# A sparse-attention and gated-feed-forward kernel on one core: conversions issued behind two copies, and the upper weight half taken first

## Chip, core and metric

The kernel runs on one core of one Trainium2 chip. The metric is device time in microseconds (us) of that core, as a median of runs; lower is better.

## What is computed

The reference is an attention with a local window and a few global keys, and a feed-forward layer with a sigmoid gate behind it. Cut to what matters:

```python
# q, k, v: (4, 8, 768, 64) fp32; n_global = 8, n_local = 96
scores = q @ k.T / sqrt(64) - slope[h] * dist      # dist by position
scores = where(is_global | is_local, scores, -1e9)
a = softmax(scores)                                # with + 1e-9 in the denominator
x = (a @ v) laid out as 3072 tokens x 512
gate = 1 / (1 + exp(-(x @ w_gate)))                # 512 x 1536
val = x @ w_val                                    # 512 x 1536
out = (gate * val) @ w_out                         # 1536 x 512
```

## The kernel before

The 3072 tokens are cut into 8 blocks of 384 (`bi` 0 to 7, three 128-token tiles `t` each), the 8 heads into 4 pairs (`s` 0 to 3), the 1536 inner columns into 12 groups of 128 (`f` 0 to 11).

**Attention of a block**, for each pair `s` and tile `t`: `scores` puts two matmuls into two PSUM banks (L373 in blocks 0 and 1), VectorE adds the distance table and takes the row's bound (L406, result in a tile `work`), ScalarE takes the exponential (L419). `transposes` turns the 128x128 probability pieces on TensorE into a bank (L452: `ps_t` and `ps_o0` in turn), and copies the bank to a tile `pT` in SBUF: in block 0 on ScalarE for t = 0 (L457), on VectorE for t = 1 and 2 (L455). `values` multiplies the three `pT` of a pair with v (L502), going through t in the order 2, 1, 0. Tiles `pT` come from a ring of three (`PTB = 3`). In block 0, `pair_out` then normalises into `hh` (L538) and splits it into a rounded `xh` and a rest `xl`; for the last pair ScalarE writes `xh` (L544) and VectorE `xl` (L545).

**Feed-forward**, `ff_in`: a group `f` has a gate half and a value half, in banks `ps_g` and `ps_u`. Each adds 12 matmuls (L564): for 4 chunks `c` of the 512 inputs the three products `w1l*xh`, `w1h*xl`, `w1h*xh`. `w1h` is the rounded upper half of the weight, `w1l` the rest. The gate half is read by ScalarE (L572, tanh), which frees `ps_g` for the next group; the value half by VectorE (L578 or L581). `ff_out` multiplies with the output weight (L604) into three banks `ps_o`.

**Weights** come as 64-bit numbers and are turned to fp32 by integer arithmetic while block 0 runs. `conv_a` issues, on ScalarE, the low bits (L192: `bits`, or `w2f` for the output weight) and two clipped parts of the high word (L199: `neg`, `top`), or for the output weight the latter on VectorE (L203, L206). `conv_b` joins them on VectorE (L180 `top`, then L212 `bits`, or L214). `conv_c` rounds the upper half on ScalarE (L235 `w1h`), and GpSimd takes the rest (L180 `w1l`). Each group f of block 0 needs its `w1h` and `w1l`.

**Order.** A program-level scheduler places instructions by its own estimate of times. `issue_after(later, earlier)` adds an order between two instructions of one engine without a wait. In `conv_a` the first instruction on ScalarE already stands behind the last exponential issued, the first on VectorE behind the last L406. All that the change touches lies in the first fifth of the run: attention of block 0 ends at about 36 us, and block 0's feed-forward, with block 1's attention between its groups, at about 135 us.

Of the kernel before, what the change touches and what calls it, by code (L numbers as in the profile page):

```python
# [28 lines left out]
def attn_moe_kernel(ctx, tc, qT, kT, v, n_global, n_local, wg, wv, wo, out, B, H, S, D):  # L29
    nc = tc.nc  # L30
    DM = H * D
    NC = DM // P
    NF = wo.shape[0] // P
    NPAIR = H // 2
    NTB = S // P
    TB = 3
# [25 lines left out]
    def issue_after(later, earlier):  # L62
        tc.add_manual_dep(
            later.ins,
            earlier.ins.name,
            mybir.DependencyInfo(mybir.DependencyClass.NoSync, mybir.DependencyReason.DATA),
            reason="issue order",
        )
# [91 lines left out]
    w1h = [wpool.tile([P, 2, NC, P], F32R, name=f"w1h{f}") for f in range(NF)]  # L160
    w1l = [wpool.tile([P, 2, NC, P], F32R, name=f"w1l{f}") for f in range(NF)]
# [17 lines left out]
    def sub(eng, out, a, b):  # L179
        eng.tensor_tensor(out, a, b, op=ALU.subtract)  # L180

    def conv_a(j):

        c = conv[j]
        raw, n = c.pop("raw"), c["n"]
        m32 = raw.bitcast(U32).rearrange("p (n t) -> p n t", t=2)[:, 0:n, 1]
        w3 = raw.rearrange("p (n f) -> p n f", f=4)[:, 1:n + 1, 0]  # L190
        c["bits"] = w2f[c["f"]] if c["i"] == 1 else wraw.tile([P, n], I32, name="bits", bufs=2)
        first = nc.scalar.activation(c["bits"], m32, AF.Copy, scale=2.0 ** -13)  # L192
        if last_exp:
            issue_after(first, last_exp[-1])
        c["top"] = top = wraw.tile([P, 2 * CW], I16, name="top", bufs=TOPB)[:, 0:n]
        neg = wraw.tile([P, 2 * CW], I16, name="neg")[:, 0:n]
        if KINDS[c["f"]][c["i"]] == "B":
            for dst, sign in ((top, 1.0), (neg, -1.0)):
                ins = nc.scalar.activation(dst, w3, AF.Relu, scale=8.0 * sign, bias=-8.0 * 14336.0)  # L199
                issue_after(ins, first)  # L200
            sub(nc.vector, top, top, neg)
        else:
            first = nc.vector.tensor_scalar(neg, w3, -18432.0, -14336.0, op0=ALU.max, op1=ALU.min)  # L203
            if last_min:
                issue_after(first, last_min[-1])
            nc.vector.scalar_tensor_tensor(top, w3, 14336.0, neg, op0=ALU.max, op1=ALU.add)  # L206

    def conv_b(j):
# [59 lines left out]
    PAIR = 1  # L268
# [11 lines left out]
    def x_of(bi):  # L280
        o, size = xslot[bi]
        return [x[:, o:o + size].rearrange("p (c n) -> p c n", c=NC) for x in xall]

    steps = {}

    KINDS = ["RR"] + ["BR"] * 11
    TOPB = 1
# [63 lines left out]
    def bank(*names):  # L351

        i = turns.get(names, 0)
        turns[names] = i + 1
        name = names[i % len(names)]
        pool = {"ps_s": ps_a, "ps_t": ps_a, "ps_v": ps_a, "ps_g": ps_gv, "ps_u": ps_gv}.get(name, ps_o)
        return pool.tile([P, 4 * P], F32, name=name)
# [82 lines left out]
    def transposes(bi, s, t):  # L440
        st = steps[bi, s]
        b, t0, nt = blocks[bi]
        n = 1 if t0 + t == 0 else 2
        sb, _ = st.pop(("s", t))
        if bi > PAIR:
            st["pT"][t] = transposes_by_dma(s, n, sb)
            return
        pt = bank("ps_t", "ps_o0") if bi < PAIR else bank("ps_t")
        pt = pt.rearrange("p (c x) -> p c x", c=4)
        for j in range(2):  # L450
            for c in range(n):
                nc.tensor.transpose(pt[:, n * j + c], sb[:, j, c * P:(c + 1) * P], ident)  # L452
        pT = spool.tile([P, 4, P], F32, name="pT", tag="pT", bufs=PTB)
        if bi < PAIR and t > 0:
            nc.vector.tensor_copy(pT[:, 0:2 * n], pt[:, 0:2 * n])  # L455
        else:
            nc.scalar.copy(pT[:, 0:2 * n], pt[:, 0:2 * n])  # L457
        st["pT"][t] = pT

    def transposes_by_dma(s, n, sb):  # L460

        m = 2 * n
        halves = late["pool"].tile([P, 2 * 4 * P], I16, name="halves")[:, 0:2 * m * P]
        words = sb[:, :, 0:n * P].bitcast(I16).rearrange("p j (x h) -> p j x h", h=2)
        for h in range(2):
            dst = halves[:, h * m * P:(h + 1) * m * P].rearrange("p (j x) -> p j x", j=2)
            nc.vector.tensor_copy(dst, words[:, :, :, h])
        turned = late["pool"].tile([P, 2 * 4, P], I16, name="turned", bufs=2)[:, 0:2 * m]
        nc.sync.dma_start_transpose(turned, halves)
        return turned  # L470
# [83 lines left out]
    def ff_in(bi, f, mid=None):  # L554
        b, t0, nt = blocks[bi]
        n = nt * P
        xh, xl = x_of(bi)
        pss = []
        for i in range(2):
            ps = ps_gv.tile([P, NB], F32, name=("ps_g", "ps_u")[i])  # L560
            k = 0
            for c in range(NC):
                for wt, xt in ((w1l, xh), (w1h, xl), (w1h, xh)):
                    nc.tensor.matmul(  # L564
                        ps[:, :n], wt[f][:, i, c], xt[:, c, :n], start=(k == 0), stop=(k == 3 * NC - 1)
                    )
                    k += 1
            pss.append(ps)
            if i == 0:
                a = mpool.tile([P, NB], F32, name="work", tag="work", bufs=WORKB)  # L570

                last_gate[:] = [nc.scalar.activation(a[:, :n], ps[:, :n], AF.Tanh, scale=0.5)]  # L572
                if mid is not None:
                    mid()
        if bi < PAIR and f < UNSPLIT:

            h = mpool.tile([P, NB], F32, name="hh", tag="hh")
            nc.vector.scalar_tensor_tensor(h[:, :n], a[:, :n], 1.0, pss[1][:, :n], op0=ALU.add, op1=ALU.mult)  # L578
            hs[bi, f] = (h,)
            return  # L580
        nc.vector.scalar_tensor_tensor(a[:, :n], a[:, :n], 1.0, pss[1][:, :n], op0=ALU.add, op1=ALU.mult)  # L581
        hh = mpool.tile([P, NB], F32R, name="hh", tag="hh")
        hl = mpool.tile([P, NB], F32R, name="hl", tag="hl")
        nc.scalar.activation(hh[:, :n], a[:, :n], AF.Copy)  # L584
        sub(nc.vector, hl[:, :n], a[:, :n], hh[:, :n])
        hs[bi, f] = (hh, hl)
# [39 lines left out]

    LEAD = 2
    EARLY = {4: (conv_a,), 6: (conv_b, conv_c)}
    AHEAD = 13
    nblk = len(blocks)  # L630
# [73 lines left out]
    for u, (bi, f) in enumerate(seq):  # L704
# [21 lines left out]
        def mid(es=group[1]):  # L726
            for e in es:
                run(*e)
            if bi == 0:
                conv_step()  # L730

        ff_in(bi, f, mid)
        for e in group[2]:
            run(*e)
# [19 lines left out]
    ps = ps_a.tile([P, 4, P], F32, name="ps_t")  # L754
# [91 lines left out]
    with fits.Else():  # L846
        with tc.For_i(0, B, 1) as b:
            for t0 in range(0, NTB, TB):
                blocks.append((b, t0, TB))
                bi = len(blocks) - 1  # L850
# [45 lines left out]
```

## Time and profile before

| | us |
|---|---|
| median of 3 runs | 738.26 |
| the 3 runs | 736.45, 738.26, 738.61 |
| span of the profiled execution, first to last instruction | 734.4 |
| median less that span | 3.86 |
| TensorE busy, of the span | 718.1 (98%) |
| TensorE weight load busy | 653.0 (89%) |
| VectorE, ScalarE, GpSimd busy | 498.8 (68%), 420.2 (57%), 219.4 (30%) |

No time of its own is listed for the profiled execution beside its span; 3.86 us is what lies around the span if that execution took the median. Matmuls are pipelined: one that shows 0.34 us is followed by the next after about 0.17 us, so a busy TensorE still hides short waits, and waits are read from the start times.

### The profile page before, as it was taken

Reading aid. Unit: us, or ns where it says so; the run is one execution under the profiler, and the core shown is the slowest. Engines: PE = TensorE matmul, PEld = TensorE weight load, DVE = VectorE, ACT = ScalarE, POOL = GpSimd, SP = SyncE. Lnnn points to the kernel's source line nnn. Section 1 sums busy time; section 2 is a strip of 40 time slices with the busy share of each in tenths; the row PEclk is TensorE's granted clock in tenths of the full one; section 3 lists DMA queues with packets and bytes.
Section 4 is the critical chain, followed back from the end, with each engine's and each line's share of the span. In section 5 each row is a group of like instructions: output and inputs, shape, how many; then the busy total and the mean of one; then the engine's idle time right before and its main releaser. Section 6 shows DMA issues by size and latency. Waiting matters only on the chain. (4 is left out here: it accounts for less than half of the span.)

```text
span 734.4 us, 12477 instructions
## 1 busy us (share of the span) xinstructions
PE 718.1 (98%) x4403; PEld 653.0 (89%) x4403; DVE 498.8 (68%) x1303; ACT 420.2 (57%) x948; POOL 219.4 (30%) x166
## 2 busy tenths in 40 slices
PE   7999999999999999999999999999999999999996
PEld 5667788999889999999999999999999999999996
DVE  7889799668877777686777868666786877321111
ACT  5789887656565555566456655655555664332222
POOL 5424345422231323223132332313233231221222
PEclk9999999999999999999999999999999999999999
DMA  8969662624437353433435442343435224010001
GB/s 249 275 194 274 189 199 59 167 61 81 106 79 159 85 106 71 100 103 68 79 80 121 110 106 63 65 122 74 96 81 110 72 47 83 16 45 1 1 0 46
DMA packets 136866, 74.27 MB, mean 101 GB/s; under 512 B 87136, under 2 KB 129120, under 8 KB 136800
## 3 DMA queue, kind: packets, MB, share of 16 engines
q1 hardware_dynamic: 136800, 73.43, 40.1%
q8 instruction: 36, 0.59, 0.3%
q14 instruction: 30, 0.25, 0.1%
HBM read 49.81 MB, written 6.29 MB: 76 GB/s over the span
## 5 line engine op out<-in xcount | busy, mean ns | idle before, releaser
L180 POOL TENSOR_TENSOR w2l<-w2f,w2h 128x512 fp32r<-128x512 f32 x89 | 122.5, 1377 | 372.8 <-ACT w2h L217 359.1
L581 DVE SCALAR_TENSOR_TENSOR work<-work,ps_u 128x384 f32<-128x384 f32 x90 | 49.8, 553 | 127.1 <-PE ps_u L564 122.1
L564 PE MATMUL ps_g<-xh,w1l 128*128 128x384 f32 x384 | 131.1, 341 | 1.0 <-ACT work L572 1.0
L564 PE MATMUL ps_u<-xh,w1l 128*128 128x384 f32 x384 | 130.9, 341 | 0.1
L564 PE MATMUL ps_g<-xl,w1h 128*128 128x384 f32 x384 | 129.6, 337 | 0.7 <-DVE xl L545 0.7
L564 PE MATMUL ps_g<-xh,w1h 128*128 128x384 f32 x384 | 129.4, 337 | 0.0
L564 PE MATMUL ps_u<-xh,w1h 128*128 128x384 f32 x384 | 129.3, 337 | 0.0
L564 PE MATMUL ps_u<-xl,w1h 128*128 128x384 f32 x384 | 129.2, 336 | 0.0
L584 ACT ACTIVATE hh<-work 128x384 fp32r<-128x384 f32 x90 | 46.9, 521 | 131.3 <-DVE work L581 131.1
L419 ACT ACTIVATE work<-work,nms 128x256 f32<-128x256 f32 (+1 forms) x192 | 92.0, 481 | 25.8 <-DVE nms L406 25.4
L604 PE MATMUL ps_o<-w2l,hh 128*128 128x512 f32 x267 | 104.9, 393 | 0.6 <-POOL w2l L180 0.5
L604 PE MATMUL ps_o<-w2h,hh 128*128 128x512 f32 x267 | 104.1, 390 | 0.0
L604 PE MATMUL ps_o<-w2h,hl 128*128 128x512 f32 x267 | 103.1, 389 | 0.0
L180 DVE TENSOR_TENSOR hl<-work,hh 128x384 fp32r<-128x384 f32 x90 | 79.6, 884 | 23.4 <-ACT hh L584 23.2
L217 ACT ACTIVATE w2h<-w2f 128x512 fp32r<-128x512 f32 x89 | 56.0, 630 | 52.3 <-PE ps_o L604 51.0
L564 PEld LDWEIGHTS ps_g<-xh,w1l 128*128 128x128 f32 x384 | 72.2, 188 | 5.1 <-issue 2.3
L564 PEld LDWEIGHTS ps_u<-xh,w1l 128*128 128x128 f32 x384 | 72.1, 188 | 3.9 <-issue 1.2
L564 PEld LDWEIGHTS ps_g<-xl,w1h 128*128 128x128 f32 x384 | 72.2, 188 | 2.6 <-DVE xl L545 1.1
L564 PEld LDWEIGHTS ps_u<-xl,w1h 128*128 128x128 f32 x384 | 72.2, 188 | 1.0
L438 DVE TENSOR_SCALAR work<-work,rc 128x256 f32<-128x256 f32 (+1 forms) x168 | 71.4, 464 | 2.0
L564 PEld LDWEIGHTS ps_g<-xh,w1h 128*128 128x128 f32 x384 | 72.2, 188 | 0.5 <-issue 0.2
L564 PEld LDWEIGHTS ps_u<-xh,w1h 128*128 128x128 f32 x384 | 72.2, 188 | 0.0
(133 smaller groups left out, 1170.0 us busy)
## 6 DMA issues: line engine op xcount, KB each, us to landing
qr<-in_qT SPq DMA_DIRECT2D x56, 192.0 KB, 3.3
kr<-in_kT SPq DMA_DIRECT2D x32, 192.0 KB, 2.7
v<-in_v SPq DMA_DIRECT2D x32, 192.0 KB, 3.6
raw<-in_w_gate SPq DMA_DIRECT2D x12, 512.0 KB, 4.3
raw<-in_w_val SPq DMA_DIRECT2D x12, 512.0 KB, 5.6
raw<-in_w_out SPq DMA_DIRECT2D x12, 512.0 KB, 3.8
out<-ost SPq DMA_DIRECT2D x24, 256.0 KB, 2.2
v<-in_v SPq DMA_DIRECT2D x16, 144.0 KB, 3.8
```

What stands on the lines that cost most here:

```text
L180: eng.tensor_tensor(out, a, b, op=ALU.subtract)
L217: ins = nc.scalar.activation(hi, w, AF.Copy)
L419: ins = nc.scalar.activation(sb[:, j, :w], sb[:, j, :w], AF.Exp, scale=-1.0, bias=nm[:, j:j + 1], accum_out=sm[:, j:j + 1])
L438: nc.vector.tensor_scalar(sb[:, j, :w], sb[:, j, :w], rc[:, j:j + 1], None, op0=ALU.mult)
L564: nc.tensor.matmul(ps[:, :n], wt[f][:, i, c], xt[:, c, :n], start=(k == 0), stop=(k == 3 * NC - 1))
L581: nc.vector.scalar_tensor_tensor(a[:, :n], a[:, :n], 1.0, pss[1][:, :n], op0=ALU.add, op1=ALU.mult)
L584: nc.scalar.activation(hh[:, :n], a[:, :n], AF.Copy)
L604: ins = nc.tensor.matmul(outs[bi][t], ht[:, t * P:(t + 1) * P], wt, start=(f == 0 and k == 0), stop=(f == NF - 1 and k == len(parts) - 1),)
```

## The change

In `conv_a` two orders are added. The first ScalarE instruction (L192) is also issued behind the copy of the transposed probabilities of block 0's last pair, tile 0. The first VectorE instruction of an output weight (L203) is also issued behind the copy of the pair before, tile 2. `transposes` notes these copies. In `ff_in`, groups 1 to 11 of block 0 run their eight `w1h` products first and the four `w1l` products after them.

```diff
         first = nc.scalar.activation(c["bits"], m32, AF.Copy, scale=2.0 ** -13)
         if last_exp:
             issue_after(first, last_exp[-1])
+        if (0, NPAIR - 1, 0) in copies:
+            issue_after(first, copies[0, NPAIR - 1, 0])
...
             if last_min:
                 issue_after(first, last_min[-1])
+            if (0, NPAIR - 2, TB - 1) in copies:
+                issue_after(first, copies[0, NPAIR - 2, TB - 1])
...
-            nc.vector.tensor_copy(pT[:, 0:2 * n], pt[:, 0:2 * n])
-        else:
-            nc.scalar.copy(pT[:, 0:2 * n], pt[:, 0:2 * n])
+            ins = nc.vector.tensor_copy(pT[:, 0:2 * n], pt[:, 0:2 * n])
+        else:
+            ins = nc.scalar.copy(pT[:, 0:2 * n], pt[:, 0:2 * n])
+        if bi < PAIR:
+            copies[bi, s, t] = ins
...
-            for c in range(NC):
-                for wt, xt in ((w1l, xh), (w1h, xl), (w1h, xh)):
-                    nc.tensor.matmul(
-                        ps[:, :n], wt[f][:, i, c], xt[:, c, :n], start=(k == 0), stop=(k == 3 * NC - 1)
-                    )
-                    k += 1
+            terms = ((w1l, xh), (w1h, xl), (w1h, xh))
+            if bi < PAIR and f > 0:
+                each = [(c, *p) for c in range(NC) for p in terms[1:]] + [(c, *terms[0]) for c in range(NC)]
+            else:
+                each = [(c, *p) for c in range(NC) for p in terms]
+            for c, wt, xt in each:
+                nc.tensor.matmul(
+                    ps[:, :n], wt[f][:, i, c], xt[:, c, :n], start=(k == 0), stop=(k == 3 * NC - 1)
+                )
+                k += 1
```

The scheduler moves more than these lines. ScalarE, at the end of block 0's attention, before; `ps_o_506` is the bank of the last pair's tile 0, `w2f_162`, `raw_377` and `w1h_139` belong to the output weight of group 0 and to group 1:

```order
L419 ACTIVATE work,sums<-work,nms 128x256
L192 ACTIVATE w2f_162<-raw_375 128x512
L192 ACTIVATE bits<-raw_377 128x1024
L199 ACTIVATE neg<-raw_377 128x1024
L199 ACTIVATE top<-raw_377 128x1024
L457 COPY pT<-ps_o_506 128x256
L536 COPY hl<-ps_o_586 128x384
L235 ACTIVATE w1h_139<-bits 128x1024
```

The same place of the change (L462 is L457 of before, L201 is L199, L239 is L235):

```order
L424 ACTIVATE work,sums<-work,nms 128x256
L462 COPY pT<-ps_o_506 128x256
L192 ACTIVATE w2f_162<-raw_375 128x512
L192 ACTIVATE bits<-raw_377 128x1024
L201 ACTIVATE neg<-raw_377 128x1024
L201 ACTIVATE top<-raw_377 128x1024
L543 COPY hl<-ps_o_586 128x384
L239 ACTIVATE w1h_139<-bits 128x1024
```

The copy has moved from behind four conversion instructions to ahead of them. VectorE at the same place, before (`pT<-ps_o_565` is the copy of the last pair's tile 2):

```order
L538 TENSOR_TENSOR hh<-ps_v,hl 128x384
L455 COPY pT<-ps_t 128x512
L180 TENSOR_TENSOR top<-top,neg 128x1024
L455 COPY pT<-ps_o_565 128x512
L212 TENSOR_TENSOR bits<-top,bits 128x1024
```

And of the change (L545 is L538 of before, L218 is L214, L460 is L455, L216 is L212):

```order
L545 TENSOR_TENSOR hh<-ps_v,hl 128x384
L218 SCALAR_TENSOR_TENSOR w2f_162<-top,w2f_162 128x512
L460 COPY pT<-ps_t 128x512
L460 COPY pT<-ps_o_565 128x512
L180 TENSOR_TENSOR top<-top,neg 128x1024
L216 TENSOR_TENSOR bits<-top,bits 128x1024
```

The copy now stands ahead of the first joining instruction, and one joining instruction of the output weight (L214 of before) has moved behind the `hh` of the pair before. TensorE around group 2 of block 0, before; `qr_547` are score matmuls of block 1's pair 1 (here tile 1), `w1l_152` and `w1h_140` the weight halves of group 2:

```order
L604 MATMUL ps_o_788<-w2f_163,hh 128x512
L373 MATMUL ps_v<-kr,qr_547 128x256
L373 MATMUL ps_s<-kr,qr_547 128x256
L564 MATMUL ps_g<-xh,w1l_152 128x384
L564 MATMUL ps_g<-xl,w1h_140 128x384
```

And of the change (L615 is L604 of before, L378 is L373, L575 is L564), with the middle of the group left out:

```order
L615 MATMUL ps_o_788<-w2f_163,hh 128x512
L575 MATMUL ps_g<-xl,w1h_140 128x384
L575 MATMUL ps_g<-xh,w1h_140 128x384
...
L575 MATMUL ps_u<-xh,w1l_152 128x384 x4
L378 MATMUL ps_v<-kr,qr_547 128x256
L378 MATMUL ps_s<-kr,qr_547 128x256
```

The score pair has moved from ahead of group 2 to behind it, and so have the score pairs that follow, each by about one group; by group 7 the two orders have met again.

## Rows read from the trace of the kernel before

**Rows 1.** The page: span, and busy time, share and instructions by engine.

```profile
span 734.4 us, 12477 instructions
PE 718.1 (98%) x4403; PEld 653.0 (89%) x4403; DVE 498.8 (68%) x1303; ACT 420.2 (57%) x948; POOL 219.4 (30%) x166
```

**Rows 2.** All waits of TensorE from 60 to 140 us: us in total, times, longest.

```profile
PE ps_o L604 <- POOL w2l L180: 0.5, 2, 0.3
PE ps_t L452 <- ACT pT L457: 0.2, 1, 0.2
```

**Rows 3.** TensorE in order, 29 to 41 us: start, us, what, idle before.

```profile
29.29 1.31 PE L502 MATMUL ps_v<-pT,v 128*64 128x128 f32 x20
...
32.61 0.66 PE L452 MATMUL ps_o<-ident,work 128*128 128x128 f32 x4 [0.61 <-ACT pT L457]
...
34.13 1.31 PE L502 MATMUL ps_v<-pT,v 128*64 128x128 f32 x20 [0.52 <-DVE pT L455]
...
38.28 0.44 PE L564 MATMUL ps_g<-xl,w1h 128*128 128x384 f32 x1 [0.74 <-DVE xl L545]
...
40.46 0.42 PE L564 MATMUL ps_g<-xh,w1l 128*128 128x384 f32 x1 [0.57 <-ACT work L572]
```

**Rows 4.** ScalarE in order, 28 to 36 us.

```profile
28.53 0.65 ACT L192 ACTIVATE w2f<-raw 128x512 int32<-128x512 uint32 x1
...
31.18 1.12 ACT L199 ACTIVATE top<-raw 128x1024 int16<-128x1024 int16 x1
32.21 0.34 ACT L457 COPY pT<-ps_o 128x256 f32<-128x256 f32 x1
32.46 0.47 ACT L536 COPY hl<-ps_o 128x384 f32<-128x384 f32 x1
35.40 1.06 ACT L235 ACTIVATE w1h<-bits 128x1024 fp32r<-128x1024 f32 x1 [2.47 <-DVE bits L212]
```

**Rows 5.** VectorE in order, 32 to 47 us.

```profile
32.33 1.14 DVE L180 TENSOR_TENSOR top<-top,neg 128x1024 int16<-128x1024 int16 x1 [0.42 <-ACT top L199]
33.40 0.68 DVE L455 COPY pT<-ps_o 128x512 f32<-128x512 f32 x1
34.00 1.31 DVE L212 TENSOR_TENSOR bits<-top,bits 128x1024 int16<-128x1024 int16 x1
...
45.36 0.69 DVE L180 TENSOR_TENSOR top<-top,neg 128x1024 int16<-128x1024 int16 x1 [0.40 <-ACT top L199]
46.09 1.31 DVE L212 TENSOR_TENSOR bits<-top,bits 128x1024 int16<-128x1024 int16 x1
```

**Rows 6.** TensorE in order, 57 to 60 us: end of group 2, scores, group 3.

```profile
57.38 0.34 PE L564 MATMUL ps_u<-xl,w1h 128*128 128x384 f32 x1
57.55 0.34 PE L564 MATMUL ps_u<-xh,w1h 128*128 128x384 f32 x1
58.73 0.48 PE L373 MATMUL ps_v<-kr,qr 64*128 64x256 f32 x1 [0.84 <-DVE nms L406]
...
59.37 0.44 PE L564 MATMUL ps_g<-xh,w1l 128*128 128x384 f32 x1
```

**Rows 7.** Windows: stretch, us, busy us (instructions) by engine, granted clock, DMA share, GB/s.

```profile
40.00:60.00 20.00, 18.70 (x92) 13.37 (x93) 18.13 (x45) 19.44 (x38) 5.27 (x4) 1.00 0.71 212
```

**Rows 8.** ScalarE at 58 us.

```profile
58.37 0.50 ACT L572 ACTIVATE work<-ps_g 128x384 f32<-128x384 f32 x1
```

**Rows 9.** GpSimd in order, 31 to 60 us and at 116 us.

```profile
31.93 1.00 POOL L180 TENSOR_TENSOR xl<-hh,xh 128x384 fp32r<-128x384 f32 x1
...
56.54 2.58 POOL L180 TENSOR_TENSOR w1l<-bits,w1h 128x512 fp32r<-128x512 f32 x2 [3.97 <-ACT w1h L235]
...
116.31 2.65 POOL L180 TENSOR_TENSOR w1l<-bits,w1h 128x512 fp32r<-128x512 f32 x2
```

**Rows 10.** A weight load: its issue, the median to landing by the page, its reader.

```profile
32.33 0.35 SPq L175 DMA_DIRECT2D raw<-in_w_gate  x1
...
raw<-in_w_val SPq DMA_DIRECT2D x12, 512.0 KB, 5.6
...
47.04 1.17 ACT L192 ACTIVATE bits<-raw 128x1024 int32<-128x1024 uint32 x1
```

**Rows 11.** VectorE at 110 and 115 us: the same operation at two lengths.

```profile
110.32 0.62 DVE L438 TENSOR_SCALAR work<-work,rc 128x256 f32<-128x256 f32 x2
...
115.30 2.51 DVE L438 TENSOR_SCALAR work<-work,rc 128x256 f32<-128x256 f32 x2
```

More of the change, by code (lines that the diff above doesn't have):

```diff
@@ L284, in attn_moe_kernel @@
     steps = {}
+    copies = {}
     KINDS = ["RR"] + ["BR"] * 11
```

## Prediction

> **What bounds the kernel.** I read the page first [rows 1]: TensorE is busy 718.1 of 734.4 us, the other engines at most 68%. The order of instructions shows that the change neither adds nor removes a matmul, so the sum of TensorE's work stays, and the time can move only by TensorE's waits in the stretch that the change reaches, about 28 to 140 us. The list of waits and TensorE in order of time give them. At the end of block 0's attention there are four: 0.61, 0.52, 0.74 and 0.57 us [rows 3]. Ahead of group 3 there is one of 0.84 us [rows 6], and from 60 to 140 us only 0.5 + 0.2 = 0.7 us [rows 2]. Together 2.44 + 0.84 + 0.7 = 3.98 us. That is all that this change can win, 0.5% of 738.26 us.
>
> The Trainium skill says in "Perfetto Trace Analysis", section "Identifying the Most-Contended Engine", that the busy share of matmuls is no measure of the distance to the limit, and that the share of weight loads is to be read instead. By it, 89% here [rows 1], 11% of the span or 81 us would be open; by the waits it is 3.98 us, and the waits decide, since weight loads that run beside matmuls leave no time on the path when they idle.
>
> Then ScalarE and VectorE, because all these waits are for them. From 40 to 60 us ScalarE is busy 19.44 of 20 us and VectorE 18.13, more than TensorE with 18.70 in ScalarE's case [rows 7]. So in the first groups TensorE does not set the pace alone: what ScalarE loses before 40 us it does not make up before 60.
>
> **First edit: conversions behind the copies.** Before, ScalarE runs four conversions from 28.53 to 32.21 and only then the copy of the last pair's tile 0 [rows 4]; TensorE waits 0.61 us for it at 32.61 [rows 3], because the bank `ps_o0` is taken. In the changed order the copy comes first. But it can't start at 28.53. It writes a tile of the ring of three, and the three tiles of the pair before are all still to be read: by the 20 matmuls that start at 29.29 and take 1.31 us [rows 3]. They read tile 2 first, with 8 of the 20 (two pieces by two heads, each in two passes). So a tile is free at 29.29 + 8/20 x 1.31 = 29.8 at the earliest, and all three at 29.29 + 1.31 = 30.6. The new wait is on ScalarE, 1.3 to 2.1 us long, and behind it stand the four conversions, then the copy `hl`, `w1h` and `xh`.
>
> The copy holds ScalarE 32.46 - 32.21 = 0.25 us. The four conversions take from 28.53 to 31.18 + 1.12 = 32.30, that is 3.77 us [rows 4]. So `top` is ready at 29.8 + 0.25 + 3.77 = 33.8 to 30.6 + 0.25 + 3.77 = 34.6, where VectorE's joining instruction L180 started at 32.33 before [rows 5].
>
> On VectorE the copy of tile 2 now stands ahead of L180, where it was behind it. Its bank is filled at 32.61 + 0.66 - 0.61 = 32.7, so it ends near 32.7 + 0.68 = 33.3 [rows 3, 5] and hides in the wait for `top`. The moved L214 fills idle time ahead of it. Before, L180 to the start of L212 took 34.00 - 32.33 = 1.67 us with the copy between; now it takes 46.09 - 45.36 = 0.73 us, as at the later place where L180 lasts 0.69 and no copy lies between [rows 5]. L180 lasts 1.14 at 32.33, while GpSimd's 1.00 us from 31.93 ran beside it [rows 5, 9], and GpSimd is through at 32.93, before the new start. L212 so starts at 34.5 to 35.3 in place of 34.00: later by 0.5 to 1.3 us.
>
> L212 releases `w1h` on ScalarE, which has waited 2.47 us for it [rows 4]; `xh`, `xl` and TensorE's matmul at 38.28 follow it one by one [rows 3]. So the 0.61 and 0.52 us go, but they are lost at 38.28, where the wait grows to 0.74 + 0.61 + 0.52 + 0.5 to 1.3 = 2.4 to 3.2 us. Net at the end of the attention: **0.5 to 1.3 us later**. I take 0.8: one free tile is enough for the copy, which speaks for the early end, but each handover between engines is left out of the sum.
>
> **Second edit: upper half first.** It costs no matmul. At group 1 it wins nothing: that group starts when the tanh has freed `ps_g`, at 40.46 [rows 3]. What moves there is the 0.8 us. At groups 2 and 3 two things change. The score pair that waited 0.84 us for VectorE now stands one group later, and at its old place an older pair stands, whose bank was read long before. So that wait goes. TensorE would be through group 2 and the score pair as before, at 57.55 + 0.17 = 57.7, plus 0.8 = 58.5. But group 3 needs `ps_g`, which the tanh of group 2 frees. On ScalarE this tanh keeps its place in the order and ran at 58.37 to 58.87 [rows 8]; ScalarE is full from 40 to 60, so it comes 0.8 later, and group 3 starts at 58.9 + 0.8 = 59.7, against 59.37 before [rows 6]. The wait has changed its name: VectorE's bound before, ScalarE's tanh now. **0.5 us of the 0.8 comes back; 0.3 us stays.** With both ends of the first edit: 0.0 to 0.8.
>
> The lower half of group 3 is what the edit takes off the path. GpSimd has it at 56.54 + 2.58 = 59.12 [rows 9], 0.25 us before its first use at 59.37. Plus 0.8 it would be 59.9, a wait of 0.2 in the old order; in the new one it is needed only after eight matmuls, which start 57.55 - 57.38 = 0.17 us apart [rows 6], so 1.4 us later, and is covered. If that cover were gone, it costs 0.2.
>
> From group 4 on, score pairs and turned pieces stand elsewhere on TensorE until group 7. Nearly 0.7 us of waits lie there, which could go or grow. I take them as unchanged. The weight load that waits for `raw` to be released by `top` is issued 1.6 to 2.4 us later; before, it was issued at 32.33, landed some 5.6 us on, and was first read at 47.04 [rows 10], so 9 us of lead cover it.
>
> **Sum.** 734.4 + 0.8 - 0.5 = 734.7 us of span. With the 3.86 us that lie between this span and the median: 738.6 us, 0.3 above the median of 738.26.
>
> **The rivals.**
>
> *Nothing holds the copy.* If a tile of the ring is free in time, because the allocation is another than I read from the code, the copy runs at 28.53, `top` is ready at 32.55, L180 starts after the copy of tile 2 at 33.3, and L212 at 34.0, as before: the first edit costs 0, the second still wins 0.5, and with the 0.7 late us gone: 734.4 - 1.2 = 733.2, time 737.1. For it speaks that TensorE's wait named in the trace is the ScalarE copy and nothing else; against it the count of three tiles. It is still within 0.3%, which is 2.2 us and about what a measurement of this kernel can tell from no change.
>
> *Faster.* To pass 2.2 us the chain through L212 must come earlier too, so that 0.74 and 0.57 shrink with the rest. With every wait of the list gone but the tanh's 0.57: 734.4 - 3.41 = 731.0, time 734.9. Against it: the copy that is moved ahead does not feed that chain.
>
> *Slower.* A VectorE operation that falls into GpSimd's `w1l` is held: the same pair of L438 takes 0.62 us at 110.32 and 2.51 us at 115.30, with GpSimd's 2.65 us from 116.31 beside it [rows 9, 11]. That is 1.9 us for one hold. Shifted orders meet different holds; if one falls on what TensorE waits for in groups 2 to 8, the score bound or the value half, and the first edit costs its 0.8 net: 734.4 + 0.8 + 1.9 = 737.1, time 741.0. It decides from a hold of 1.4 us at the upper end on. Against it: such operations had some us of lead before, and TensorE shows only 0.7 us of waits there [rows 2].
>
> The Trainium skill has in "SBUF — State Buffer", section "Who interferes with whom", that VectorE and GpSimd share one pair of ports as a lock, and that the second to come stands still until the first is through; the two lengths of L438 fit that, and by it this rival is a matter of where the orders meet.
>
> **How the numbers follow.** Chances: the sum as forecast, 0.0 to 0.8 us of span later, 0.55; nothing holds the copy 0.24; the change does nothing that shows, 738.3, 0.03; faster as above 0.08; slower as above 0.10. The predicted time is the likeliest, 738.6. The first three are all within 0.3%: 0.82. The range is to leave out no more than 2 in 10: from 736.4, the case without a hold (737.1) with the 0.74 us wait gone as well, to 740.5, the slower case with a hold of 1.4 in place of 1.9 us.
>
> **What would show it.** In the profile of the changed kernel: ScalarE idle for 1.3 to 2.1 us ahead of the copy of `ps_o0`, released by TensorE's L502; no wait of TensorE at the turned pieces ahead of 32.5 us, and at `xl` a wait of over 2 us; group 1 starting near 41.3 in place of 40.46; no wait for VectorE's bound ahead of group 3, and one for the tanh in its place, group 3 starting near 59.7. I am wrong if the copy shows no wait, if L212 starts at 34.0 or sooner, or if new waits of TensorE between 60 and 140 us add up to more than 2 us.

## The result, and the profile after

The changed kernel takes **745.04 us** (median of 6 runs, 742.21 to 746.74); the kernel before, beside it, 737.36 us (6 runs, 735.52 to 738.61). The ratio is **1.0095 [1.0071, 1.012]**, by which 7.0 us are lost. Forecast was 738.6, no change that can be measured. The changed kernel was run a second time with the experiments (below, `e5_after_again`): 1.0102 [1.0071, 1.0133]. The profile taken there is called the second execution here.

The page of the kernel after, against [rows 1]: the same 4403 matmuls, a span 10.5 us longer. PEclk is the granted TensorE clock in 40 slices of the span.

```profile
span 744.9 us, 12465 instructions
PE 724.8 (97%) x4403; PEld 657.7 (88%) x4403; DVE 498.9 (67%) x1303; ACT 419.4 (56%) x948; POOL 220.4 (30%) x166
PEclk9989999999999999999999999999999999999998
```

The third slice is short of full clock. Windows of the kernel after (stretch, us, busy us by engine, granted clock, DMA share, GB/s) show where:

```profile
28.00:37.90 9.90, 7.99 (x78) 5.84 (x77) 6.28 (x11) 6.21 (x10) 2.80 (x3) 1.00 0.74 223
38.00:44.80 6.80, 6.06 (x19) 4.95 (x19) 4.65 (x16) 4.39 (x13) 1.85 (x2) 0.50 0.27 66
44.80:123.30 78.50, 73.03 (x410) 55.88 (x410) 62.49 (x129) 65.75 (x124) 28.20 (x20) 1.00 0.65 201
123.30:126.70 3.40, 3.40 (x9) 2.57 (x9) 3.40 (x7) 1.85 (x3) 2.71 (x2) 0.50 0.39 142
```

Two stretches at 0.50, the lower of the two levels (1.2 GHz): 6.8 us at 38 and 3.4 us at 123. Nothing in the forecast allowed for that: before, the profile has 1.00 from 28 to 140 us. TensorE in order of time, kernel after, against [rows 3]:

```profile
33.03 1.31 PE L509 MATMUL ps_v<-pT,v 128*64 128x128 f32 x20 [0.44 <-DVE pT L460]
...
36.29 0.48 PE L378 MATMUL ps_v<-kr,qr 64*128 64x256 f32 x1 [1.05 <-DVE hh L545]
...
37.41 0.44 PE L575 MATMUL ps_g<-xh,w1l 128*128 128x384 f32 x1 [0.42 <-ACT xh L551]
...
38.77 0.69 PE L575 MATMUL ps_g<-xl,w1h 128*128 128x384 f32 x1 [0.74 <-DVE xl L552]
39.25 0.53 PE L575 MATMUL ps_g<-xh,w1h 128*128 128x384 f32 x1
39.57 0.53 PE L575 MATMUL ps_u<-xl,w1h 128*128 128x384 f32 x1
```

Three waits within some three us, then the matmul at 38.77 lasts 0.69 in place of 0.44, and the next ones start 0.32 us apart in place of 0.17. The Trainium skill, "TensorE: Matmul & The Clock Gate", section "What's actually happening", has it that the gate lets through half or all of the pulses, and that activity is what opens it; the doubled spacing at 0.50 agrees.

ScalarE in order, kernel after, against [rows 4]:

```profile
29.66 0.37 ACT L462 COPY pT<-ps_o 128x256 f32<-128x256 f32 x1 [1.36 <-PE ps_v L509]
...
35.89 1.06 ACT L239 ACTIVATE w1h<-bits 128x1024 fp32r<-128x1024 f32 x1 [1.79 <-DVE bits L216]
```

The copy waits 1.36 us for the `values` matmuls, as forecast.

This one profile also holds something that the second execution doesn't (nor does that one have the stretch at 0.50 near 38 us): at 58.27 ScalarE waited 3.31 us for the load `raw<-in_w_out`, which landed 7.7 us after its issue, the tanh came late, and TensorE waited 3.22 us at group 3. So the second execution is the better witness for the rest. TensorE in order, second execution of the changed kernel:

```profile
29.40 1.31 PE L509 MATMUL ps_v<-pT,v 128*64 128x128 f32 x20
...
36.76 0.48 PE L378 MATMUL ps_v<-kr,qr 64*128 64x256 f32 x1 [1.07 <-DVE hh L545]
...
41.32 0.45 PE L575 MATMUL ps_g<-xl,w1h 128*128 128x384 f32 x1 [0.49 <-ACT work L583]
...
59.48 0.45 PE L575 MATMUL ps_g<-xl,w1h 128*128 128x384 f32 x1 [0.87 <-ACT work L583]
...
119.20 0.80 PE L615 MATMUL ps_o<-w2l,hh 128*128 128x512 f32 x1 [2.25 <-POOL w2l L180]
119.79 0.63 PE L615 MATMUL ps_o<-w2h,hh 128*128 128x512 f32 x1
120.22 0.63 PE L615 MATMUL ps_o<-w2h,hl 128*128 128x512 f32 x1
```

Up to group 3, at 59.48, the groups start where the forecast put them. Then comes one wait of 2.25 us at group 8, for GpSimd's `w2l`, and behind it matmuls 0.43 us apart, where before they stood 0.23 to 0.24 apart.

### The profile page after: what moved, and what is told of

Same layout as the page of the kernel before. It is cut to its first block, busy times and chain, and to the rows that moved or that the text cites. A ratio compares the mean times of both kernels' runs of the same rounds, so it can differ in the third digit from the quotient of the medians.

```text
span 744.9 us, 12465 instructions
## 1 busy us (share of the span) xinstructions
PE 724.8 (97%) x4403; PEld 657.7 (88%) x4403; DVE 498.9 (67%) x1303; ACT 419.4 (56%) x948; POOL 220.4 (30%) x166
## 5 line engine op out<-in xcount | busy, mean ns | idle before, releaser
L575 PE MATMUL ps_g<-xl,w1h 128*128 128x384 f32 x384 | 131.9, 343 | 4.0 <-ACT work L583 3.2
L575 PE MATMUL ps_g<-xh,w1h 128*128 128x384 f32 x384 | 130.2, 339 | 0.0
L575 PE MATMUL ps_u<-xl,w1h 128*128 128x384 f32 x384 | 129.6, 338 | 0.0
L575 PE MATMUL ps_u<-xh,w1h 128*128 128x384 f32 x384 | 129.5, 337 | 0.0
L575 PE MATMUL ps_g<-xh,w1l 128*128 128x384 f32 x384 | 125.6, 340 | 0.9 <-ACT work L583 0.5
L575 PE MATMUL ps_u<-xh,w1l 128*128 128x384 f32 x384 | 125.5, 340 | 0.4 <-DVE work L592 0.4
L615 PE MATMUL ps_o<-w2l,hh 128*128 128x512 f32 x267 | 105.6, 396 | 3.0 <-POOL w2l L180 2.9
L615 PE MATMUL ps_o<-w2h,hh 128*128 128x512 f32 x267 | 104.8, 392 | 0.0
L615 PE MATMUL ps_o<-w2h,hl 128*128 128x512 f32 x267 | 104.5, 392 | 0.0
L180 DVE TENSOR_TENSOR hl<-work,hh 128x384 fp32r<-128x384 f32 x90 | 76.9, 854 | 23.1 <-ACT hh L595 23.0
L575 PEld LDWEIGHTS ps_g<-xl,w1h 128*128 128x128 f32 x384 | 72.8, 190 | 8.6 <-ACT work L583 4.6
L575 PEld LDWEIGHTS ps_u<-xh,w1l 128*128 128x128 f32 x384 | 71.6, 188 | 4.4 <-issue 1.2
L443 DVE TENSOR_SCALAR work<-work,rc 128x256 f32<-128x256 f32 (+1 forms) x168 | 73.3, 475 | 2.0
L575 PEld LDWEIGHTS ps_g<-xh,w1l 128*128 128x128 f32 x384 | 72.1, 189 | 2.9 <-ACT work L583 0.9
L575 PEld LDWEIGHTS ps_u<-xl,w1h 128*128 128x128 f32 x384 | 72.3, 188 | 1.4 <-DVE work L592 0.3
L575 PEld LDWEIGHTS ps_g<-xh,w1h 128*128 128x128 f32 x384 | 72.9, 190 | 0.8 <-issue 0.4
L474 DVE COPY halves<-work 128x512 int16<-128x512 int16 (+1 forms) x144 | 61.7, 471 | 17.1 <-DMA turned<-halves 15.6
```

Of the source, the lines that this page charges most:

```text
L443: nc.vector.tensor_scalar(sb[:, j, :w], sb[:, j, :w], rc[:, j:j + 1], None, op0=ALU.mult)
L575: nc.tensor.matmul(ps[:, :n], wt[f][:, i, c], xt[:, c, :n], start=(k == 0), stop=(k == 3 * NC - 1))
L615: ins = nc.tensor.matmul(outs[bi][t], ht[:, t * P:(t + 1) * P], wt, start=(f == 0 and k == 0), stop=(f == NF - 1 and k == len(parts) - 1),)
```

## The experiments

Each ratio is against runs of the kernel before on the same chip (medians 736.91, 738.05, 738.52 and 737.05 us in the four sets); an amount in us is the ratio's excess times that median.

### The edits one by one

`e1_scalar_only` keeps of the change only the order on ScalarE, `e2_vector_only` only that on VectorE, `e4_terms_only` only the second edit.

```diff
+        if (0, NPAIR - 1, 0) in copies:                    # e1
+            issue_after(first, copies[0, NPAIR - 1, 0])
...
+            if (0, NPAIR - 2, TB - 1) in copies:           # e2
+                issue_after(first, copies[0, NPAIR - 2, TB - 1])
...
+            if bi < PAIR and f > 0:                        # e4
+                each = [(c, *p) for c in range(NC) for p in terms[1:]] + [(c, *terms[0]) for c in range(NC)]
```

> Only the ScalarE half of the first edit: the conversions wait for the copy of the last pair's turned probabilities; TensorE's rows stand as before in the opening. Theory A (the second edit cost the 7.7 us: TensorE's new order makes its waits longer, the granted clock falls, the tanh comes late): within 0.3% of before, 0.5 to 1 us above it (group 1 starts some 0.5 us later), granted clock 1.00 from 30 to 130. Theory B (the first edit makes a conversion late, with it the loads of weights behind it, and the tanh ahead of group 3): 3 us or more above before, and a TensorE wait of over 2 us for the tanh near 60.

> Only the VectorE half of the first edit. Both theories: within 0.3% of before, since the one conversion that moves stands behind one copy of 0.69 us; TensorE's rows are those of before.

> Only the second edit: TensorE's rows are exactly those of the changed kernel. Theory A: 5 to 8 us above before (0.7 to 1.1%), with a stretch of granted clock 0.50 near 38 to 45 and a wait for the tanh ahead of group 3. Theory B: within 0.3% of before, clock 1.00.

> The changed kernel once more, for a second profile. If the low clock near 38 to 45 and the 3.2 us wait for the tanh belong to the order of the work, both are here again, and the time is 1.0095 of before within its interval; if they were a chance of one execution (a slow load), one of them is missing and the time stands nearer to before.

| | median us (runs) | ratio | us |
|---|---|---|---|
| e1, ScalarE order | 740.67 (12) | 1.0038 [1.0018, 1.0058] | +2.8 |
| e2, VectorE order | 736.79 (12) | 1.0008 [0.999, 1.0026] | +0.6 |
| e4, second edit | 742.12 (6) | 1.0065 [1.0041, 1.0089] | +4.8 |
| e5, all | 744.69 (6) | 1.0102 [1.0071, 1.0133] | +7.5 |

The parts add up to 8.2, against 7.0 and 7.5 measured for the whole: both edits cost, the first by its ScalarE half (e2 can't be told from no change), and the second, forecast at a gain of 0.5, costs most. e5 has nearly the ratio of the first runs, and its profile, without the low clock near 38 us and without the 3.22 us wait, still has a span 6.9 us longer than before, so these two are not the main cost. Theory A comes near with the size of e4 (4.8 us for 5 to 8), but not with the place: e4 has its low clock at 118 us, and e1 has one too, at 42. Theory B falls with e4. The list of waits of TensorE from 60 to 225 us in e4:

```profile
PE ps_o L611 <- POOL w2l L180: 3.0, 2, 2.2
PE ps_s L388 <- DVE ks L180: 1.2, 1, 1.2
PE ps_g L571 <- ACT work L579: 0.5, 1, 0.5
PE ps_u L571 <- DVE work L588: 0.4, 1, 0.4
```

And the same list of the kernel before:

```profile
PE ps_s L387 <- DVE ks L180: 1.2, 1, 1.2
PE ps_o L604 <- POOL w2l L180: 0.5, 2, 0.3
PE ps_g L564 <- ACT work L572: 0.5, 1, 0.5
PE ps_t L452 <- ACT pT L457: 0.2, 1, 0.2
```

5.1 less 2.4 is 2.7 us of new waits, nearly all for `w2l`. The windows of e4 give the rest:

```profile
118.10:121.50 3.40, 3.40 (x9) 2.63 (x9) 3.40 (x7) 1.86 (x3) 2.72 (x2) 0.50 0.39 146
```

3.4 us at half clock cost half of that, 1.7. Together 4.4 us, against 4.8 by the ratio and 5.1 by the spans (739.5 and 734.4). So the place of most of e4's loss in the trace is known; not of all, since e4 starts group 3 at 58.10, 1.27 us ahead of the kernel before, and so loses 6.4 us of span behind it. Whether that wait is the cause is another question, to which e8, e13 and e14 go.

### Does the clock cost the rest of the first edit?

`e9_scalar_held` is e1 with four matmuls of zeros, 128 columns each, added into `ps_g` where TensorE waits 1.05 us for `hh`; the sums stay.

```diff
+    HOLD = {9: 4}
...
+                if bi < PAIR and f == 0 and i == 0 and k in HOLD:
+                    for _ in range(HOLD[k]):
+                        nc.tensor.matmul(ps[:, :P], zeros.to_broadcast([P, P]), zeros.to_broadcast([P, P]), start=False, stop=False)
```

> The ScalarE half of the first edit, and four matmuls of zeros (128 columns, added into a sum that they do not change) ahead of the score pair that waits 1.05 us for hh; the order of everything else is that of the run with this half alone. If the first edit costs by the clock that its waits pull down: granted clock 0.996 or more in nearly all executions, no stretch at 0.50 between 35 and 50, time 737 to 738.5, 2 us under the run with this half alone. If it costs by the waits themselves: 740 as there.

Measured 737.63 us (12 runs), 1.0011 [0.9995, 1.0028], +0.8 us where e1 has +2.8. Windows of e1, at the place of the waits:

```profile
41.70:48.50 6.80, 6.26 (x19) 5.18 (x20) 4.64 (x16) 4.62 (x14) 1.62 (x2) 0.50 0.17 45
```

And of e9:

```profile
38.00:45.00 7.00, 5.67 (x33) 4.42 (x33) 5.81 (x21) 5.66 (x15) 1.89 (x2) 1.00 0.33 88
```

e1 gets 19 matmul records in 6.8 us, e9 33 in 7.0. So about 2 us of the first edit are clock. The 0.8 us left agree with the waits of the forecast, but can't be told from nothing (the interval is -0.4 to 2.1 us). The two intervals overlap a little; that the low stretch is gone from the profile carries the reading. Five of e1's runs have a mean clock of 0.988 or less, and its profile shows another low stretch, near the start (last section), which the edit doesn't touch. Without the runs of 0.993 or less on either side, e1 stands 2.2 us above the kernel before and e9 0.2 us below, so the difference stays.

### Where does the second edit cost?

`e6_terms_1_5` makes it in groups 1 to 5 alone, `e7_terms_6_11` in 6 to 11 alone.

```diff
-            if bi < PAIR and f > 0:
+            if bi < PAIR and 0 < f < UNSPLIT:      # e6; e7: f >= UNSPLIT, which is 6
```

> The second edit in groups 1 to 5 alone; ScalarE's, VectorE's and the queues' rows differ from before nearly as in the run with the whole second edit, TensorE's groups 6 to 11 keep the old order of terms. Theory C1 (the second edit costs because the new order of ScalarE puts a conversion ahead of the split of the output weights of group 8, so that TensorE waits 2.2 us for the low half and then runs 3.4 us at clock 0.50): 3 to 5 us above before, ratio 1.004 to 1.007, wait of about 2 us for w2l near 117. Theory C2 (it costs because groups 6 to 11 reach their output products at another time): within 0.3% of before or faster, no such wait.

> The second edit in groups 6 to 11 alone: only TensorE's rows differ from before (66 rows), the other engines issue in the old order. Theory C1: within 0.3% of before, wait for w2l at group 8 near the 0.3 us of before. Theory C2: 3 to 5 us above before.

e6: 742.98 us (6 runs), 1.0081 [1.0059, 1.0103]. e7: 738.97 us (12 runs), 1.0017 [1.0002, 1.0033]. The cost comes with groups 1 to 5, where score pairs, conversions and with them all engines' orders move. But e6 doesn't show the 2.2 us at group 8, so theory C1 has the groups right and the wait wrong. TensorE in order, e6:

```profile
102.55 0.44 PE L571 MATMUL ps_g<-xh,w1l 128*128 128x384 f32 x1 [0.88 <-POOL w1l L180]
...
168.96 0.44 PE L571 MATMUL ps_u<-xh,w1l 128*128 128x384 f32 x1 [2.39 <-DVE work L588]
...
170.69 0.52 PE L571 MATMUL ps_u<-xh,w1h 128*128 128x384 f32 x1
```

Much the same price is paid at other places: 0.88 at group 8, 1.6 for `w2l` in two waits (0.66 and 0.95), and 2.39 at 169 with the low clock behind it.

That e7's 1.2 us come from its edit isn't shown. Up to 62 us all its engines run in the order of the kernel before, and yet TensorE waits longer ahead of group 3, 1.86 us in place of the 0.84 of [rows 6]. VectorE in the kernel before, then VectorE, TensorE and a window of e7:

```profile
56.28 1.71 DVE L438 TENSOR_SCALAR work<-work,rc 128x256 f32<-128x256 f32 x2
...
56.28 2.68 DVE L439 TENSOR_SCALAR work<-work,rc 128x256 f32<-128x256 f32 x2
...
59.70 0.48 PE L374 MATMUL ps_v<-kr,qr 64*128 64x256 f32 x1 [1.86 <-DVE nms L407]
...
60.70:64.10 3.40, 3.40 (x12) 3.08 (x10) 3.37 (x10) 2.39 (x4) 0.93 (x1) 0.50 1.03 346
```

GpSimd's `w1l` began at 56.54 before and at 56.07 in e7, where it ran beside both operations of the pair and not beside one. ScalarE's conversions ahead of it had begun 0.53 us earlier (53.18 against 53.71); in the kernel before they had waited 0.38 us there for a weight load. So the 0.84 us is one execution's number: e2, e9 and e11, with the same order of TensorE at this place, show 1.83 to 1.93 us.

### The wait for w2l: mended at three ends

The chain at group 8 in e4, GpSimd, VectorE and TensorE in order of time, one after the other:

```profile
110.57 1.34 POOL L180 TENSOR_TENSOR w1l<-bits,w1h 128x512 fp32r<-128x512 f32 x1
115.10 2.71 POOL L180 TENSOR_TENSOR w2l<-w2f,w2h 128x512 fp32r<-128x512 f32 x1 [3.20 <-ACT w2h L217]
...
115.50 0.58 DVE L180 TENSOR_TENSOR hl<-work,hh 128x384 fp32r<-128x384 f32 x1
115.97 0.71 DVE L206 SCALAR_TENSOR_TENSOR top<-raw,neg 128x512 int16<-128x512 int16 x1
116.78 1.63 DVE L214 SCALAR_TENSOR_TENSOR w2f<-top,w2f 128x512 int16<-128x512 int16 x1
...
117.86 0.61 PE L611 MATMUL ps_o<-w2l,hh 128*128 128x512 f32 x1 [2.21 <-POOL w2l L180]
```

The subtraction takes 2.71 us, twice the 1.34 of the row above it. In the kernel before, the same two rows:

```profile
114.56 1.79 POOL L180 TENSOR_TENSOR w2l<-w2f,w2h 128x512 fp32r<-128x512 f32 x1 [6.55 <-ACT sm L432]
...
116.40 0.50 PE L604 MATMUL ps_o<-w2l,hh 128*128 128x512 f32 x1 [0.32 <-POOL w2l L180]
```

So it starts 0.54 later and lasts 0.92 longer, and TensorE is there 0.43 earlier (117.86 - 2.21 = 115.65 against 116.40 - 0.32 = 116.08): 1.89, which is 2.21 - 0.32.

`e13_split_first`, e4 with one more edit, lets ScalarE take `w2h` ahead of the next conversion at groups 8 and 9, so that GpSimd starts earlier.

```diff
+        if last_split:
+            issue_after(first, last_split[-1])
...
-        if bi < PAIR:
-            conv_until(2 * f + 1)
         if bi >= PAIR or f >= UNSPLIT:
             split_w2(f, u == len(seq) - 1)
+        if bi < PAIR:
+            conv_until(2 * f + 1)
```

> The second edit alone, and on ScalarE the split of the output weights of groups 8 and 9 ahead of one conversion (w2f) that stood before it; two swaps of neighbours, nothing else moves on any engine. Theory S (the 2.21 us wait for w2l is made up of that conversion, 0.56 us, of a GpSimd subtraction that took 2.71 in place of 1.79 us, and of TensorE coming 0.43 us earlier): the split starts 0.56 us earlier, the wait falls to 1.65 us or less, and the time by 0.5 to 1 us, to about 741.3; more, up to 2.3 us, where the shorter wait leaves the clock at 1.00. Theory D (the wait is only where TensorE gives back what it gained up to there): the wait shrinks but the next groups wait for as much more; 742.

Measured 740.91 us (12 runs), 1.005 [1.0034, 1.0067]; e4's 1.0065 lies inside. GpSimd and TensorE in order, e13:

```profile
114.57 3.27 POOL L180 TENSOR_TENSOR w2l<-w2f,w2h 128x512 fp32r<-128x512 f32 x1 [2.63 <-ACT w2h L219]
...
117.89 0.66 PE L616 MATMUL ps_o<-w2l,hh 128*128 128x512 f32 x1 [2.25 <-POOL w2l L180]
```

The start came 0.53 earlier and the end didn't: 117.84 against 117.81. So, as far as this pair of runs shows, VectorE sets the end: in both runs its operations stand beside the subtraction with gaps of some 0.1 us at most, and at nearly the same times (115.97 and 116.78 above are 116.01 and 116.82 in e13). Theory S expected a wait of 1.65 us or less and falls. The Trainium skill, "SBUF — State Buffer", section "Who interferes with whom", says that a VectorE instruction with two SBUF inputs contends with GpSimd's reads, and that the order of issue decides who blocks. The contention agrees (the subtraction at 1.34, 2.71 and 3.27 us, and L214 at 1.63 where the kernel before has 0.75); that the order of issue decides doesn't show here.

`e8_low_last` and `e14_wait_filled` are e4 with one more edit each: e8 puts the three `w2l` products of group 8 last in its output step, e14 puts two matmuls of zeros, 512 columns each, into the wait.

```diff
+        if bi < PAIR and f == 8:                                        # e8
+            parts = (parts[1], parts[2], parts[0])
+            each = [(t, k) for t in range(nt) for k in (0, 1)] + [(t, 2) for t in range(nt)]
...
+        if bi < PAIR and f == 8:                                        # e14
+            for _ in range(2):
+                ins = nc.tensor.matmul(
+                    outs[bi][0][:, 0:512], zeros.to_broadcast([P, P]), zeros.to_broadcast([P, 512]), start=False, stop=False
+                )
...
```

> The whole second edit, with the three products of group 8 that read the low half w2l put behind the six that read the high half; nothing else in any engine's order differs from the run with the second edit alone. Six products of 0.23 us now lie ahead of the wait: it should fall from 2.2 us to about 0.85. If the wait is the cost and pulls the clock down: 1.4 us less than the second edit alone, and 3 us less where the clock then stays at 1.00. If the wait only marks a delay that is owed elsewhere: the time of the second edit alone, about 742.

> The second edit alone, and two matmuls of zeros (512 columns each, added into a sum that they do not change) in the wait for w2l at group 8; a few rows of later groups change places. If the 3.4 us at clock 0.50 behind this wait are the wait's doing: the clock stays at 1.00 there, and the time falls by some 1.7 us against the second edit alone, to 740.4. If the clock falls there anyway, the time stays at 742 or rises.

e8: 741.16 us (11 runs), 1.0047 [1.0031, 1.0064]. TensorE waits at 60 to 140 us, e8:

```profile
PE ps_o L615 <- POOL w2l L180: 1.6, 2, 1.3
PE ps_g L571 <- ACT work L579: 0.8, 1, 0.8
PE ps_u L571 <- DVE work L588: 0.5, 1, 0.5
PE ps_o L615 <- DVE hl L180: 0.3, 1, 0.3
```

The wait for `w2l` at group 8 is down to 0.33 us and the clock stays at 1.00, but 2.4 us of waits stand at groups 8 to 10 in its place (the 0.8 is group 3's). About 1.3 us come back by the ratios, not the 3 expected for a clock at 1.00 nor 4.8; the intervals of e4 and e8 overlap.

e14: 746.5 us (6 runs), 1.0104 [1.0074, 1.0133]. Windows of e14, the place of the wait and a later one:

```profile
118.00:140.00 22.00, 20.80 (x106) 17.29 (x105) 17.63 (x22) 14.56 (x25) 13.82 (x9) 1.00 0.29 72
174.80:178.10 3.30, 3.30 (x13) 3.30 (x13) 0.98 (x4) 0.47 (x2) 0.00 (x0) 0.50 0.96 193
```

The zeros did what they were for: 0.53 us of wait left, and full clock behind it. But later rows of the engines' orders moved with it (21 matmuls by the two traces), and a wait of 2.40 us stands at 174.01, for a value half as in e6, with a low stretch behind it. The expected gain didn't come.

`e15_after_mended` is the changed kernel with the zeros of e9 and the order of e13.

> The changed kernel with the four matmuls of zeros of the run that held the clock in the opening, and the split of the output weights ahead of the conversion. If the two costs are apart and add: 744.8 - 2.5 (clock in the opening) - 0.6 (split) = 741.7, granted clock 0.996 or 0.997 in most executions. If the second edit's cost hides the first one's: 743.5 or more.

745.45 us (6 runs), 1.0113 [1.0085, 1.0141]: no gain. Group 1 starts at 40.79 with full clock, but `w2l` still makes TensorE wait 2.20 us (GpSimd's subtraction lasts 3.26), and the wait near 170 is there too, with 2.35 us.

### Is it the conversions that come late?

A rival theory: score pairs that move later on TensorE make the exponentials late, and the conversions that stand behind the last exponential with them. `e10_terms_unpinned` is e4 without that order from the ninth conversion (group 4) on; `e12_both_unpinned` also without VectorE's; `e11_before_unpinned` is the control, the kernel before with the change of e10.

```diff
-        if last_exp:
+        if last_exp and j < 8:      # e10 on e4, e11 on the kernel before
...
-            if last_min:
+            if last_min and j < 8:  # e12 as well
```

> The second edit alone, and from group 4 on the first ScalarE conversion of a weight is no longer held behind the exponentials of the last score pair. Theory P (the second edit moves the score pairs of the next block to a later place among TensorE's groups; the conversions are held in order behind their exponentials, so they come 4 to 6 us later at groups 5 and 6, VectorE idles 5.5 of the 20 us from 60 to 80, and TensorE pays for it later, at whatever it then waits for): the conversions of groups 4 to 6 start within 2 us of before, VectorE is busy 16 us or more from 60 to 80, and 3 us or more of the 4.5 come back: 737 to 739.5. Theory W (the cost is the waits of TensorE that the new order of its own rows makes): 741 to 743 as with the second edit alone.

> The control: the kernel before, with the same order rule taken away and nothing else. Theory P: the rule costs little there, since the score pairs come early; within 0.5% of before, on either side. Theory W: no statement. If this kernel gains 3 us as well, what the run with the second edit gains says nothing on its cause.

> The second edit alone, and from group 4 on neither ScalarE's nor VectorE's first conversion is held behind the last score pair. Theory P: at least as much comes back as with ScalarE's rule alone, 736.5 to 739.5. Theory W: 741 to 743.

| | median us (runs) | ratio |
|---|---|---|
| e10 | 741.23 (11) | 1.0039 [1.0023, 1.0056] |
| e11 | 745.38 (6) | 1.0104 [1.0073, 1.0136] |
| e12 | 745.35 (6) | 1.0092 [1.0071, 1.0112] |

The theory falls. In e12 the gate and value weights of groups 4 to 6 began to be converted 0.2 to 1.1 us earlier than before the change and those of groups 7 to 11 4.3 to 9.2 us earlier (in e4 up to 4.8 us later), and it cost 0.92%. e10 stays in the range that theory W gave, 741 to 743 us. TensorE's longest waits at 60 to 140 us in e12:

```profile
PE ps_s L388 <- POOL qs L180: 2.8, 1, 2.8
PE ps_g L571 <- ACT work L579: 1.0, 2, 0.8
```

And the control e11 has none of the change and lost 1.04%, with a wait of 1.91 us at 126.72 (`xl`) and low clock behind it. Its 1.83 us at 62.68, for VectorE's bound, is the wait ahead of group 3 that e7 and e2 show too, and four of its six runs have a mean clock of 0.990 or less, so the size of its loss is less sure than its sign. Four orders of the same work, e4, e6, e11 and e12, each cost 0.7 to 1.0%, and their profiles show other waits in each. The order before is a good one, but not the only one: e2, with four VectorE rows in other places, and e7, with the second edit in half the groups, cost 0.1 and 0.2%.

## Why the prediction was wrong, point by point

**First edit, in its own waits: right.** The copy was released by the `values` matmuls, 1.36 us late (forecast 1.3 to 2.1). It started 0.70 after they began (29.66 against 28.96; forecast 0.5 to 1.3): one free tile is enough. Group 1 stands at 41.32 in the second execution (forecast 41.3); counted from the `values` matmuls it is 11.92 us against 11.17 before, 0.75 later for a forecast of 0.8. One thing stood elsewhere: I put the whole wait at `xl`, 2.4 to 3.2 us. It came in pieces, 1.05 at the score pair that needs the bank `ps_v` read by `hh`, 0.42 at `xh`, 0.74 at `xl` as before. I had left out that `hh` stands behind L216 on VectorE. And the 0.52 us ahead of the last `values`, which I let go, stayed as 0.44.

**What the first edit's sum left out: the clock.** The three waits close together were followed by 6.8 us at 0.50 in the profiles of after and of e1, not in the second execution; e9 puts the price at about 2 us in the median of e1. The two runs of the changed kernel agree: of their 12 executions four have the mean clock of the first profile, 0.991, and take 745.9 us in the median, seven have 0.994 or 0.995, as the second execution, and take 744.2. The forecast had no term and no rival for it.

**Second edit up to group 3: right.** The 0.84 us wait for VectorE's bound is gone, one of 0.87 for the tanh is there, and group 3 starts at 59.48 (forecast 59.7). From the `values` matmuls that is 30.08 us, as before to the hundredth, for a forecast of 0.3 later; in e4, without the first edit, it is 29.31, 0.8 us won where I had 0.5. That it fits so closely is partly luck: e7, in the order of before, took 31.11.

**The step that failed** is the sentence "From group 4 on, score pairs and turned pieces stand elsewhere on TensorE until group 7. ... I take them as unchanged." 0.7 us of waits there became 2.2 in the second execution, one wait for `w2l` with 3.4 us of low clock behind it. In e4's trace new waits and low clock make 4.4 us, where the ratio has 4.8. By the sign that I had set, new waits of more than 2 us from 60 to 140, this term is refuted. A reading was wrong as well: I wrote that all waits are for ScalarE and VectorE, but 0.5 of these 0.7 us were for GpSimd's `w2l` [rows 2], the very wait that grew. I saw that the orders meet again on TensorE by group 7 and took that for the end of it. The other engines' orders were still shifted against each other, and the wait came at group 8.

**The rivals.** The slower one had the right mechanism, GpSimd and VectorE in each other's way, and the right sign: 741.0 us with the first edit, by a hold of 1.9 us. At group 8 the sides were swapped: I had a VectorE operation held up by GpSimd [rows 11]; here GpSimd's subtraction was held up by VectorE. As I had worded it, on the score bound or the value half, it stands in e7 ahead of group 3, and in block 1, near 170 us, in e6, e14 and e15. The wait at group 8 was 2.2 us, and the clock behind it added 1.7. What spoke against it, 0.7 us of waits in the old order, is no evidence on a new order. *Nothing holds the copy* is refuted by the 1.36 us, *faster* by every run, and *nothing shows* by the ratio.

**The sum's base.** The 3.86 us that I set around the span were too many: the profiled runs of after and of e5 show 746.74 - 744.9 = 1.84 and 743.07 - 741.3 = 1.77. That profiled execution was some 2 us faster than the median. It would have moved the forecast by nothing that counts. A slip of 0.1 us changes as little: by the forecast's own rows the weight load is issued 1.5 to 2.3 us later, not 1.6 to 2.4.

**What stays open.** Which of the shifted orders makes `w2l` late first is only argued. Taking that wait away gave back 1.3 us of 4.8 (e8) or nothing (e14), since others took its place, so that this wait is the cause of e4's loss isn't shown. Why the wait of 2.4 us near 170 shows in e6, e14 and e15 and is 0.4 in e4 is found in part. VectorE in e6, then in e4:

```profile
164.49 1.54 DVE L486 COPY pT<-turned 128x512 int16<-128x512 int16 x1
...
164.37 0.46 DVE L486 COPY pT<-turned 128x512 int16<-128x512 int16 x1
```

In e6 GpSimd's subtraction `qs` runs beside this copy, and its `w2l` beside the `ks` subtraction behind it (1.61 us in place of 0.62): holds of 2.1 us, against 1.5 in e4. The rest, some 1.5 us by which VectorE stands later against TensorE, wasn't traced; there `pT` comes by a DMA transpose of `halves`, and VectorE waits on those. The late load in the profile of after looks like chance: in the other 15 profiles the same load landed 3.6 to 5.7 us after its issue, in the second execution 4.4. No version that was run beats the kernel before; e2 and e9 can't be told from it.

## What to carry to other kernels

A tuned order has only small waits because its engines happen to fit, so "0.7 us of waits in that stretch" says what a change can win there and nothing on what it can lose: where an edit shifts all engines' orders, expect a new wait somewhere in the stretch, past the point where the orders on one engine meet again (here seven of the fourteen kernels other than the one before show one of 2.2 to 2.8 us between 100 and 175 us). And read a wait from more than one execution: the 0.84 us of the trace before were 1.86 in e7, in the same order. Price a new wait of TensorE with what the clock may do after it: here a wait of 2.2 us and the low clock behind it are 3.9 us in the trace. Filling a wait with matmuls of zeros keeps the clock up (e9, e14), but only where the wait is the end of the matter does it win time.

## What the runs showed of the hardware

**The clock after a wait.** Waits of TensorE of 2.20 to 2.25 us for `w2l` (after, e4, e5, e13, e15), of 2.39 (e6) and of 2.40 us (e14) were each followed, 0 to 1.2 us later, by 3.4 us at 0.50. So were 1.81 (e10), 1.86 (e7) and 1.91 us (e11, at 126.72); beside one of 2.76 us (e12) stood 6.8 us of it, as beside three waits of 0.42 to 1.05 us in a row (e1, after). It isn't certain: 1.83 us (e2, and e11 at 62.68), 1.93 (e9), 2.35 (e15, at 171.15) and 3.22 us (after, ahead of 63.49) were followed by full clock, and so were the same three short waits in the second execution.

**A hold between GpSimd and VectorE.** A VectorE pair of operations of 0.35 us each (L438) took 1.71 us with GpSimd beside the second (kernel before) and 2.68 with GpSimd beside both (e7). A GpSimd subtraction of 128x512 took 1.34 us where VectorE was the one held, and 2.71 and 3.27 beside a row of VectorE operations (e4, e13).

**The clock near the start.** In the profiles of e1, e8, e11 and e14 some 10.2 us at 0.50 stand between 10.9 and 21.9 us, in stretches that those edits don't touch; other profiles have none. Over the runs of the kernel before, 20 of 84 in the four sets have a mean clock of 0.993 or less and take 738.44 to 741.0 us; 29 have 0.999 or more and take 735.06 to 737.73. That is most of its spread. That the 20 hold this stretch is inferred: 10.2 us at half clock take 0.007 off the mean, and no profile of the kernel before fell on such an execution.
